# An adaLN block with dilated local attention and a SwiGLU FFN: the second gate moved from w2 to the output tiles, and a new order of all queues

## The chip, the cores and the metric

The kernel runs on one core of one Trainium2 chip. The metric is the device time of one execution in microseconds, as the median over several runs. Before the change it is 240.24 us (three runs, 239.44 to 240.56).

## The reference

`x` is 2048 tokens by 512 features, in bf16. A condition vector `c` gives six modulation rows of 512; a LayerNorm without weights, scaled and shifted, stands ahead of the attention and ahead of the FFN, and each branch is added with a gate.

```python
sa, ca, ga, sb, cb, gb = silu(c) @ w_mod            # six rows of 512
h = layernorm(x) * (1 + ca) + sa
x = x + ga * attention(h, wqkv, wo)
h = layernorm(x) * (1 + cb) + sb
x = x + gb * ((silu(h @ w1) * (h @ w3)) @ w2)       # w1, w3: 512x1792, w2: 1792x512
```

The attention has 32 heads of width 16. Token s sees the 8 tokens s, s-2, ..., s-14; those before token 0 are masked.

## The kernel before

**Tiles.** The tokens are 16 tiles of 128. Weights stay in SBUF. The LayerNorm and projections of the first half run over groups of tiles `LN1 = [[0,1],[2,3],[4..7],[8..11],[12..15]]`, the attention over pairs of tiles, the FFN over groups `FFN = [[0,1],[2,3],[4..7],[8..11],[12,13],[14,15]]`. A group has 256 or 512 tokens.

**The first half.** `ln_stats` takes mean and variance of a tile on VectorE (L555, L556), adds epsilon, raises to -0.5 on POOL (L565) and normalises on VectorE (L576; tile 0 alone by a broadcast operand, L571). In the first group each of the two tiles has its own chain. `ln_T` transposes by TensorE (L636) or, for later groups, by DMA, and applies scale and shift while it evicts to h (L644 on ScalarE, L651 on VectorE, L621 behind a DMA transpose). `proj_qk` and `proj_v` project (L691, L711); for a group with `vh.pieces` each of the four blocks of features is an operation by itself, which can start on its piece of h. v goes to DRAM, so that shifted rows can be loaded.

**Attention of a pair.** `logits`: one VectorE product of 128x4096 per tile (pq, L742) and its sum over features by TensorE (L752). `shift`, `exps`, `softmax`: maximum, exponentials, sum, reciprocal and weights, on VectorE and ScalarE (L764 to L797), and a transpose of the weights (L807, called at). `values`: four loads of shifted v (256 KB each, called vl), one VectorE product of 128x4096 (av, L827), a sum by TensorE (L855, called ac), a copy (L861), a DMA transpose (ot), the output projection with the scaled wo (L867, called wo), and the residual addition, which leaves the row sum too (L871, called rs).

**The FFN.** `ln_sums`: minus the mean on POOL (L586), a Square with its sum on ScalarE per tile (L590), variance, power and bias on POOL (L596, L597, L599), a normalise on ScalarE per tile (L601). `ffn_unit(f)`: gate product (L883), Silu (L889), up product (L883), product of both (hh, L892, VectorE). The text calls these units f0 to f83: 14 per group, f0 to f13 for tiles 0 and 1, f14 to f27 for tiles 2 and 3, f28 to f41 and f42 to f55 for the two groups of 512 tokens, and so on. Units of two groups are interleaved. `ffn_w2` sums over the 14 blocks in two halves of 7 (z0 and z1 are the halves of tile 0, z2 and z3 of tile 1), for the last two tiles in two column halves instead (L909). `store` adds x from PSUM (L931, called zo) and writes out.

**The gates.** ga is multiplied into wo once (L946). gb is multiplied into w2 once, in four parts (L952), so that the w2 sum needs no more than the addition of x.

**What sets the order.** Every operation is recorded first, with its readers and writers. `ORDER` is a written list of all operations; `place` splits it into the queue of each engine, and each engine executes its queue in that order. `SLOTS` gives each temporary its buffer: PSUM banks (8), shifted-v buffers (three with the one that lies over wqkv), products, hidden blocks. A reader waits on its writers by semaphores, and a new tenant of a buffer on the users of the old one. SP issues almost all the DMAs, in its own queue. PSUM banks are so few that a gate or up product must often wait until the bank's tenant two or three units earlier has been read.

Of the kernel before, what the change touches and what calls it, by code (L numbers as in the profile page):

```python
# [7 lines left out]
ALU = mybir.AluOpType  # L8
# [264 lines left out]
def _build(p, A_x, A_wqkv, A_wo, B_w1, B_w3, B_w2, c, w_mod, out):  # L273
# [275 lines left out]
    def ln_stats(Ts):  # L549
# [15 lines left out]
        p.op("pool", lambda e: e.tensor_tensor(rsn, rsn, bass.AP(cst, 1, [[2, P], [0, n]]), ALU.pow), 600, k, r=[va, vcst],  # L565
             w=[vr])
        vns = []
        for T in Ts:
            vn = Val("xn", xnpool)
            if T == 0:  # L570
                p.op("dve", lambda e, vn=vn, T=T: e.scalar_tensor_tensor(vn.at[:], x_sb[:, T, :], mv[:, T, 0:1], bass.AP(rs, T, [[2 * NT, P], [0, D]]),  # L571
                                                                         op0=ALU.subtract, op1=ALU.mult), 600, ("nm", T),
                     r=[vx[T], vr] + vms, w=[vn])
                vns.append(vn)
                continue
# [33 lines left out]
    def ln_T(which, gi, vns):  # L609
        vh = Val("h", hpool)  # L610
        vh.pieces = [Val(f"h_{ft}") for ft in range(KT)] if not which and not gi else None
# [15 lines left out]
        for half in range(2):  # L627
# [12 lines left out]
            for j in range(2):  # L640
# [233 lines left out]
    vw2s = [Val(f"w2_scaled{g}") for g in range(NG)]  # L874
# [24 lines left out]
    def ffn_w2(T, tt, vhh, zops):  # L899

        if T >= NT - 2:
            n = D // 2
            for q in range(2):
                vz = Val("ps_z", psum)
                o = None
                for a, c in ((0, 10), (10, NF)):
                    def mm(e, q=q, vz=vz, a=a, c=c):
                        for fi in range(a, c):
                            ins = e.matmul(bank(vz)[:, 0:n], vhh[fi].at[:, tt * P:(tt + 1) * P], w2[:, fi, q * n:(q + 1) * n],  # L909
# [3 lines left out]
                    o = p.op("pe", mm, (c - a) * c_mm(n), ("z", 2 * T + q), r=vhh[a:c] + vw2s[0 if a == 0 else 2:3 if a == 0 else 4], part=[vz], after=[o] if o else [])  # L913
# [4 lines left out]
        for q in range(2):  # L918
# [6 lines left out]
            o = p.op("pe", mm, 7 * MM, ("z", 2 * T + q), r=vhh[7 * q:7 * q + 7] + vw2s[2 * q - (q > 0):2 * q + 2], part=[vz], after=[o] if q else [])  # L925
            zops[q].append(o)
        store(T, 0, D, vz)
# [10 lines left out]
    for gi, Ts in enumerate(LN1):  # L938
        vns = [v for pr in ([[T] for T in Ts] if gi == 0 else pairs(Ts)) for v in ln_stats(pr)]
# [10 lines left out]
    for g in range(NG):  # L950
        a, b = cuts[g], cuts[g + 1]
        p.op("dve", lambda e, a=a, b=b: e.tensor_tensor(w2[:, a:b, :], w2[:, a:b, :],  # L952
                                                      bass.AP(gb_bc, 0, [[D, P], [0, b - a], [1, D]]), ALU.mult),
             48 + 274 * (b - a), ("mod", 7 + g), r=[vw2[g], vg[1]], w=[vw2s[g]], lock=True)
# [8 lines left out]
    for gi, Ts in enumerate(FFN):  # L963
        vns = [v for pr in pairs(Ts) for v in ln_sums(pr)]
# [112 lines left out]
```

## Time and profile before

| | us |
|---|---|
| median of three runs | 240.24 |
| the runs | 239.44, 240.24, 240.56 |
| span of the profiled execution, first to last instruction | 237.7 |
| TensorE matmuls, busy union | 229.7 |
| VectorE | 179.4 |
| ScalarE | 138.5 |
| POOL | 29.2 |

The profiled execution is recorded as its span alone, 237.7 us; the median of the runs stands 2.5 above it. Where the text works with the span, it adds these 2.5 at the end. The page of the profile lists busy time per engine, the chain of work that ended last, and groups of instructions by source line; the windows give busy time per stretch, and the timeline gives starts and lengths. A row of the timeline reads: start, length, engine, line, operation, tiles, count, and in brackets the idle time before it and who ended it.

### The profile page before, as it was taken

To read this page: it belongs to the slowest core of one execution; us is meant where nothing else is said; L and a number is where in the kernel's file an instruction comes from. 1 tells how busy PE (TensorE), PEld (TensorE's weight loads), DVE (VectorE), ACT (ScalarE), POOL (GpSimd) and SP (SyncE) were. 2 spreads that over 40 slices of the span, in tenths; PEclk is the share of its full clock that TensorE was granted. 3 is DMA by queue.
4 is the path that set the end of the run, shared out by engine and by line. 5 is a ranking of instruction groups with operands and counts; after the bars stand their busy time and mean duration, and the time that the engine had idled before them with its cause. 6 is when DMAs were issued, how large, how long until landed. Compare 5 with 4: busy or idle time off the path is not lost.

```text
span 237.7 us, 4535 instructions
## 1 busy us (share of the span) xinstructions
PE 229.7 (97%) x1781; PEld 136.2 (57%) x1806; DVE 179.4 (75%) x279; ACT 138.5 (58%) x267; POOL 29.2 (12%) x66
## 2 busy tenths in 40 slices
PE   7999999999999998999999999999999999999995
PEld 4776454445588674664444444444475457485774
DVE  5699999999999989999999999682654403434433
ACT  2289577999978744985865594837473405040300
POOL 4434100013002000240002520012010000000000
PEclk9999999999999999999999999999999999999999
DMA  6999999999999999897981693642203000000202
GB/s 216 372 337 322 158 237 299 208 269 283 353 200 270 243 249 199 173 260 177 247 234 47 182 234 72 154 132 46 67 19 91 3 0 0 6 19 0 70 0 88
DMA packets 46317, 38.85 MB, mean 163 GB/s; under 512 B 21704, under 2 KB 37080, under 8 KB 46296
## 3 DMA queue, kind: packets, MB, share of 16 engines
q1 hardware_dynamic: 46288, 38.56, 66.9%
q8 instruction: 14, 0.23, 0.4%
q14 instruction: 7, 0.06, 0.1%
q10 hardware_dynamic: 8, 0.00, 0.0%
HBM read 29.62 MB, written 4.21 MB: 142 GB/s over the span
## 4 chain that ended last, share of the span: by engine, by line
PE 74%; DMA 8%; DVE 8%; SPq 4%; ACT 3%; issue 2%; ACTq 0%; DVEq 0%
PE pall L883 38%; PE pall L921 18%; DMA sb_x<-in_A_x_dram 5%; PE pall L867 5%; SPq L124 4%; PE pall L691 4%; DMA sb_vsh<-v_scratch_dram 3%; PE pall L909 3%; PE pall L855 2%; PE pall L752 2%; PE pall L711 2%; DVE sb_vsh L827 2%; DVE sb_pq L742 2%; DVE sb_hh L892 1%; ACT sb_h L621 1%
## 5 line engine op out<-in xcount | busy, mean ns | idle before, releaser
L883 PE MATMUL pall<-sb_h,sb_w 128*128 128x256 bf16 (+1 forms) x664 | 101.9, 307 | 1.8 <-DVE sb_hh L892 0.9
L883 PEld LDWEIGHTS pall<-sb_h,sb_w 128*128 128x128 bf16 x672 | 64.8, 98 | 37.2 <-issue 2.8
L889 ACT ACTIVATE sb_sg<-pall 128x256 bf16<-128x256 f32 (+1 forms) x84 | 35.6, 453 | 54.1 <-PE pall L883 53.0
L892 DVE TENSOR_TENSOR sb_hh<-sb_sg,pall 128x256 bf16<-128x256 bf16 (+1 forms) x84 | 39.9, 505 | 34.8 <-PE pall L883 32.7
L921 PE MATMUL pall<-sb_w,sb_hh 128*128 128x512 bf16 x190 | 44.0, 379 | 0.3
L742 DVE TENSOR_TENSOR sb_pq<-sb_q,sb_kT 128x4096 bf16<-128x4096 bf16 x16 | 36.3, 2282 | 0.0
L921 PEld LDWEIGHTS pall<-sb_w,sb_hh 128*128 128x128 bf16 x196 | 19.0, 98 | 21.6 <-DVE sb_hh L892 0.4
L691 PE MATMUL pall<-sb_h,sb_wqkv 128*128 128x512 bf16 (+1 forms) x154 | 30.2, 335 | 0.5 <-issue 0.2
L827 DVE TENSOR_TENSOR sb_vsh<-sb_vsh,sb_al 128x4096 bf16<-128x4096 bf16 x12 | 27.3, 2287 | 2.1 <-DMA sb_vsh<-v_scratch_dram 2.1
L621 ACT ACTIVATE sb_h<-sb_h,sb_modc 128x512 bf16<-128x512 bf16 (+1 forms) x24 | 16.5, 743 | 10.1 <-DMA sb_h<-sb_xn 10.1
L691 PEld LDWEIGHTS pall<-sb_h,sb_wqkv 128*128 128x128 bf16 x160 | 14.7, 98 | 11.8 <-ACT sb_ac L861 0.4
L931 DVE TENSOR_TENSOR sb_o<-pall,sb_x 128x512 bf16<-128x512 f32 (+1 forms) x18 | 11.1, 625 | 10.5 <-PE pall L921 6.8
L711 PE MATMUL pall<-sb_wqkv,sb_h 128*128 128x512 bf16 x62 | 15.5, 379 | 0.2
L867 PE MATMUL pall<-sb_wo,sb_ot 128*128 128x512 bf16 x61 | 15.3, 379 | 0.3 <-issue 0.2
L586 POOL TENSOR_SCALAR sb_nm<-sb_sx 128x2 f32<-128x2 f32 x8 | 1.7, 218 | 105.2 <-DVE sb_x L871 105.1
L644 ACT ACTIVATE sb_h<-pall,sb_modc 128x256 bf16<-128x256 bf16 (+1 forms) x18 | 9.9, 612 | 7.5 <-DVE sb_modc L509 6.5
L861 ACT ACTIVATE sb_ac<-pall 128x512 bf16<-128x512 f32 x16 | 9.5, 595 | 7.2 <-PE pall L855 7.1
L601 ACT ACTIVATE sb_xn<-sb_x,sb_nb,sb_rs 128x512 bf16<-128x512 bf16 x16 | 12.4, 806 | 0.7 <-POOL sb_nb L599 0.6
L871 DVE SCALAR_TENSOR_TENSOR sb_x<-pall,sb_x 128x512 bf16<-128x512 f32 x16 | 10.9, 686 | 1.5 <-PE pall L867 1.3
L590 ACT ACTIVATE sb_xn<-sb_x,sb_nm 128x512 bf16<-128x512 bf16 x16 | 11.4, 714 | 0.7 <-POOL sb_nm L586 0.7
L721 ACT ACTIVATE sb_v<-pall 128x512 bf16<-128x512 f32 x16 | 9.5, 600 | 2.8 <-PE pall L711 2.8
L555 DVE BATCH_NORM_STATS2 sb_st<-sb_x 128x6 f32<-128x512 bf16 x16 | 10.6, 680 | 0.8 <-DMA sb_x<-in_A_x_dram 0.7
(87 smaller groups left out, 208.3 us busy)
## 6 DMA issues: line engine op xcount, KB each, us to landing
sb_vsh<-v_scratch_dram SPq DMA_DIRECT2D x48, 256.0 KB, 5.5
sb_vshx<-v_scratch_dram SPq DMA_DIRECT2D x16, 256.0 KB, 4.6
sb_w<-in_B_w_dram SPq DMA_DIRECT2D x6, 512.0 KB, 7.9
sb_w<-in_B_w_dram SPq DMA_DIRECT2D x6, 384.0 KB, 5.4
v_scratch_dram<-sb_v SPq DMA_DIRECT2D x16, 128.0 KB, 6.4
out_dram<-sb_o SPq DMA_DIRECT2D x14, 128.0 KB, 1.8
sb_wqkv<-in_A_wqkv_dram SPq DMA_DIRECT2D x6, 256.0 KB, 6.3
sb_x<-in_A_x_dram SPq DMA_DIRECT2D x4, 256.0 KB, 6.4
```

The source lines that it names most:

```text
L590: p.op("act", lambda e, vn=vn, T=T: e.activation(vn.at[:], x_sb[:, T, :], ACT.Square, bias=nm[:, T, :], accum_out=var[:, T, :]), c_act(512 ...
L601: p.op("act", lambda e, vn=vn, T=T: e.activation(vn.at[:], x_sb[:, T, :], ACT.Identity, bias=nb[:, T, :], scale=rs[:, NT + T, :]), c_act(5 ...
L621: return e.activation(vh.at[:, ft, 0:n * P], vh.at[:, ft, 0:n * P], ACT.Identity, bias=modc[:, 8 * which + ft:8 * which + ft + 1], scale=m ...
L691: ins = e.matmul(bank(vp)[:, j * n:(j + 1) * n], wqkv[:, t, col:col + P], vh.at[:, t, 0:n], start=(t == ORDER[0] and j == 0), stop=(t == O ...
L711: ins = e.matmul(bank(vp), vh.at[:, t, tt * P:(tt + 1) * P], wqkv[:, t, 2 * D:3 * D], start=(t == ORDER[0]), stop=(t == ORDER[-1]))
L742: return e.tensor_tensor(vp.at[:], in0, in1, ALU.mult)
L827: return e.tensor_tensor(v_w, v_w, a_w, ALU.mult)
L867: ins = e.matmul(bank(vy), vt.at[:, ft, :], wo[:, ft, :], start=(ft == 0), stop=(ft == KT - 1))
L883: ins = e.matmul(bank(vp)[:, 0:n], wt[:, t, fi * P:(fi + 1) * P], vh.at[:, t, 0:n], start=(t == 0), stop=(t == KT - 1))
L889: p.op("act", lambda e: e.activation(vt.at[:, 0:n], bank(vgp)[:, 0:n], ACT.Silu), c_act(n), k, r=[vgp], w=[vt], table="silu")
L892: p.op("dve", lambda e: e.tensor_tensor(vh_.at[:, 0:n], vt.at[:, 0:n], bank(vup)[:, 0:n], ALU.mult), c_dve(n), k, r=[vt, vup], w=[vh_])
L921: ins = e.matmul(bank(vz), vhh[fi].at[:, tt * P:(tt + 1) * P], w2[:, fi, :], start=(fi == 0), stop=(fi == NF - 1))
```

## The change

The multiply of w2 by gb is taken out. For tiles 0 to 13 the finished w2 sum is copied from PSUM by ScalarE, multiplied by gb and added to x on VectorE, both in bf16 in SBUF. For the last two tiles two scaled copies of w2 (blocks 0 to 7 and 8 to 13) are made late, in two shifted-v buffers that are free by then. The first pair of tiles has one joint chain for its statistics, and the second pair's projections are cut by pieces too, with two of its evictions on VectorE.

```diff
-        vns = [v for pr in ([[T] for T in Ts] if gi == 0 else pairs(Ts)) for v in ln_stats(pr)]
+        vns = [v for pr in pairs(Ts) for v in ln_stats(pr)]
...
-            if T == 0:
-                p.op("dve", lambda e, vn=vn, T=T: e.scalar_tensor_tensor(vn.at[:], x_sb[:, T, :], mv[:, T, 0:1], bass.AP(rs, T, [[2 * NT, P], [0, D]]),
-                                                                         op0=ALU.subtract, op1=ALU.mult), 600, ("nm", T),
...
-        vh.pieces = [Val(f"h_{ft}") for ft in range(KT)] if not which and not gi else None
+        vh.pieces = [Val(f"h_{ft}") for ft in range(KT)] if not which and gi < 2 else None
...
-                if not half and not which and gi < 1:
+                if not half and not which and gi < 2:
                     p.op("dve", ev_dve, c_dve(n * P), k, r=[vt, vmod[which][2 * half + j]], part=[vh, vh.pieces[2 * half + j]])
...
-    vw2s = [Val(f"w2_scaled{g}") for g in range(NG)]
+    w2v = [Val(f"w2_scaled{i}", vshpool) for i in range(2)]
...
+            def scaled(fi, q):
+                return w2v[fi // 8].at[:, fi % 8, q * n:(q + 1) * n]
...
-                            ins = e.matmul(bank(vz)[:, 0:n], vhh[fi].at[:, tt * P:(tt + 1) * P], w2[:, fi, q * n:(q + 1) * n],
+                            ins = e.matmul(bank(vz)[:, 0:n], vhh[fi].at[:, tt * P:(tt + 1) * P], scaled(fi, q),
...
-        store(T, 0, D, vz)
+        vo = Val("o", opool)
+        k = ("zo", T)
+        p.op("act", lambda e: e.activation(vo.at[:], bank(vz), ACT.Copy), c_act(512), k, r=[vz], w=[vo])
+        o = p.op("dve", lambda e: e.tensor_tensor(vo.at[:], vo.at[:], gb_bc[:], ALU.mult), 340, k, r=[vg[1]], w=[vo], lock=True)
+        p.op("dve", lambda e: e.tensor_tensor(vo.at[:], vo.at[:], x_sb[:, T, :], ALU.add), 340, k, r=[vx[T]], w=[vo], lead=o, lock=True)
+        finals.append(p.dma(out2d[T * P:(T + 1) * P, :], lambda: vo.at[:], k, (128, 1024), r=[vo], cost=400, store=True))
...
-    for g in range(NG):
-        a, b = cuts[g], cuts[g + 1]
-        p.op("dve", lambda e, a=a, b=b: e.tensor_tensor(w2[:, a:b, :], w2[:, a:b, :],
-                                                      bass.AP(gb_bc, 0, [[D, P], [0, b - a], [1, D]]), ALU.mult),
-             48 + 274 * (b - a), ("mod", 7 + g), r=[vw2[g], vg[1]], w=[vw2s[g]], lock=True)
...
+        if Ts[-1] == NT - 1:
+            for i, (a, b) in enumerate(((0, 8), (8, NF))):
+                p.op("dve", lambda e, i=i, a=a, b=b: e.tensor_tensor(w2v[i].at[:, 0:b - a, :], w2[:, a:b, :],
+                                                                     bass.AP(gb_bc, 0, [[D, P], [0, b - a], [1, D]]), ALU.mult),
+                     48 + 274 * (b - a), ("mod", 7 + i), r=vw2 + [vg[1]], w=[w2v[i]], lock=True)
```

`ORDER` and `SLOTS` are new as a whole. Read as queues, SP issues its transfers in the old order up to the third part of w3 (load 19); behind that, and on TensorE, VectorE, ScalarE and POOL, the order differs. The parts of the new queues that the prediction uses:

| tiles | VectorE behind the residual, before | after | TensorE from the last output projection of the group's tiles to its first gate product, after |
|---|---|---|---|
| 0, 1 | sm2 sum, sm2 reciprocal, sm2 weights, sm4 sum, pq7, pq6 | sm2 sum, reciprocal, weights, pq7, pq6 | q17 k16 k17 v13 at2 q16 k18, transposes, k19, transposes, q19 v14 q18, f1 |
| 2, 3 | sm6 weights, w2 scaling, f12 f7 f8 f9 f11 f13, av5 | f5 f12 f10 f3 f11 f9, pq9, f8 f7, pq8 | at6 f12 f12 f10 f3 f9 f9 f8 f7 f8, z2, transposes, f13, z0, f24 |
| 6, 7 | sm8 weights, f18 f14, pq11 | f19 f22, pq11, f24 f27, pq10 | at8 f22 f24 z3 f27 f27 z6 z7 z4 z5 lg10 lg11 ac9 ac8, f32 |
| 8, 9 | f39 f36, av11 | pq15, pq14 | (tiles 10, 11 close the group) f30 f30 f40 f34 wo10 wo11 lg15 lg14 f28 f31 follow wo9 |
| 12, 13 | f48, av14 | zo3, f53, zo0, av14 | f53 f43 f45 f43 f51 f45 f52 ac14 f47 f47 z9 z11 z13, f59 |

Here q, k, v with a number are projections, lg the logits of a tile, sm the softmax steps of a pair.

More of the change, by code (lines that the diff above doesn't have):

```diff
@@ L908, in mm @@
                         for fi in range(a, c):
[L909 removed]
+                            ins = e.matmul(bank(vz)[:, 0:n], vhh[fi].at[:, tt * P:(tt + 1) * P], scaled(fi, q),
                                            start=(fi == 0), stop=(fi == NF - 1))
                         return ins
[L913 removed]
+                    o = p.op("pe", mm, (c - a) * c_mm(n), ("z", 2 * T + q), r=vhh[a:c] + (w2v if a == 0 else w2v[1:]), part=[vz], after=[o] if o else [])
                 store(T, q * n, n, vz)
@@ L923, in mm @@
                 return ins
-            o = p.op("pe", mm, 7 * MM, ("z", 2 * T + q), r=vhh[7 * q:7 * q + 7] + vw2s[2 * q - (q > 0):2 * q + 2], part=[vz], after=[o] if q else [])
+            o = p.op("pe", mm, 7 * MM, ("z", 2 * T + q), r=vhh[7 * q:7 * q + 7] + vw2[2 * q - (q > 0):2 * q + 2], part=[vz], after=[o] if q else [])
             zops[q].append(o)
-        store(T, 0, D, vz)
+        vo = Val("o", opool)
[4 more added lines that the diff above has]
+        finals.append(p.dma(out2d[T * P:(T + 1) * P, :], lambda: vo.at[:], k, (128, 1024), r=[vo], cost=400, store=True))
     def store(T, c0, n, vz):
```

5 lines of the change are left out of this document (1 added, 4 removed), and 134 rows, old and new, of tables (ORDER, SLOTS).

## The prediction

> **What bounds the kernel now.** I read the busy line of the page first, then the windows of 10 us, then the chain of waits, then the timeline at the stalls.
>
> ```profile
> PE 229.7 (97%) x1781; PEld 136.2 (57%) x1806; DVE 179.4 (75%) x279; ACT 138.5 (58%) x267; POOL 29.2 (12%) x66
> ```
>
> ```profile
> 0.00:10.00 10.00, 8.07 (x79) 5.70 (x80) 6.84 (x26) 2.16 (x3) 4.42 (x20) 1.00 0.84 283
> ...
> 80.00:90.00 10.00, 9.13 (x99) 6.44 (x88) 8.82 (x9) 4.31 (x11) 0.00 (x0) 1.00 1.17 239
> 90.00:100.00 10.00, 9.59 (x70) 5.19 (x70) 9.86 (x19) 7.49 (x14) 0.62 (x4) 1.00 0.80 183
> ...
> 170.00:180.00 10.00, 9.95 (x69) 6.67 (x69) 4.46 (x11) 7.67 (x17) 1.31 (x4) 1.00 0.14 45
> ...
> 230.00:238.00 8.00, 5.02 (x47) 4.26 (x44) 2.30 (x5) 0.00 (x0) 0.00 (x0) 0.99 0.21 66
> ```
>
> TensorE is the bound, at full clock (the 1.00), and the change takes no matmul from it. It is idle 8.0 us of 237.7: 1.9 in the first 10 us, 3.0 after the last matmul, 1.3 between 80 and 100, and 1.8 in all the rest. So what can be won is small: the 1.3 us, part of the start, a few tenths. What can be lost is not bounded: TensorE executes its queue in the order that was written, and every late operand is a hole. The chain gives the prices of its work:
>
> ```profile
> 79.47 0.55 PE pall L752 x16
> 80.03 0.43 PE pall L855 x6
> 80.46 0.22 PE pall L636 x2
> 80.67 1.51 PE pall L921 x7
> 82.19 2.62 PE pall L883 x24
> ```
>
> A gate or up product of a 256-token group (4 matmuls) takes 2.62/6 = 0.44, one of a 512-token group 4 x 1.51/7 = 0.86, a half w2 sum 1.51, a logits or value reduction 0.55 each (0.43 x 8/6 for the latter). The 1.3 us look like this in the timeline:
>
> ```profile
> 87.14 2.29 DVE L827 TENSOR_TENSOR sb_vsh<-sb_vsh,sb_al 128x4096 bf16<-128x4096 bf16 x1 [1.04 <-DMA sb_vsh<-v_scratch_dram]
> 89.36 1.40 DVE L892 TENSOR_TENSOR sb_hh<-sb_sg,pall 128x256 bf16<-128x256 bf16 x4
> 89.82 1.05 PE L883 MATMUL pall<-sb_h,sb_w 128*128 128x256 bf16 x8 [0.87 <-DVE sb_hh L892]
> ```
>
> VectorE waited 1.04 for a shifted-v load, four SwiGLU products stood behind that multiply, and TensorE had no free PSUM bank for 0.87 us. Rows on such loads, and on the issue of two transposes, are needed below:
>
> ```profile
> sb_vsh<-v_scratch_dram SPq DMA_DIRECT2D x48, 256.0 KB, 5.5
> ...
> sb_w<-in_B_w_dram SPq DMA_DIRECT2D x6, 384.0 KB, 5.4
> ```
>
> ```profile
> 166.63 2.58 SPq L124 DMA_TRANSPOSE sb_h<-sb_xn  x2
> ```
>
> **The change part by part.**
>
> ```profile
> L952 DVE TENSOR_TENSOR sb_w<-sb_w,sb_gb_bc 128x2048 bf16<-128x2048 bf16 (+1 forms) x4 | 4.3, 1084 | 0.0
> ...
> L931 DVE TENSOR_TENSOR sb_o<-pall,sb_x 128x512 bf16<-128x512 f32 (+1 forms) x18 | 11.1, 625 | 10.5 <-PE pall L921 6.8 <-PE pall L909 3.8
> ...
> L742 DVE TENSOR_TENSOR sb_pq<-sb_q,sb_kT 128x4096 bf16<-128x4096 bf16 x16 | 36.3, 2282 | 0.0
> ...
> L861 ACT ACTIVATE sb_ac<-pall 128x512 bf16<-128x512 f32 x16 | 9.5, 595 | 7.2 <-PE pall L855 7.1
> ```
>
> *Scaling and stores.* The four L952 multiplies (4.3 us, between 68 and 96 us) leave VectorE where it is full; two multiplies over the same 14 blocks return after the last value multiply, again about 4.3, on an engine that is busy 4.5 of 10 us there. For 14 tiles one add from PSUM becomes a ScalarE copy (0.60, the L861 row) and two bf16 operations of 512: a line through the products (4096 wide, 2282 ns) and the mean scaling (1792 wide, 1084 ns) gives 152 ns fixed and 266 per 512, so 0.42 each. So VectorE gets 14 x (0.84 - 0.62) = 3.1 us and ScalarE 14 x 0.60 = 8.4 us more, nearly all after 105 us, where both have room: no cost by themselves (if a copy stands ahead of a needed Silu, 0.6 a time). The multiply of 2.2 us in front of f60's product holds PSUM banks, but four 512-token products (3.5 us) lie in TensorE's queue for that time. The SP queue has the same stores; the first, zo0, stands ahead of the transposes tr18, and its data are there before theirs. At the end zo13's copy, multiply and add lie beside the last 56 half-width matmuls, and the final add and store are unchanged: nothing.
>
> *Start.* Both first tiles now share one power; the broadcast normalise of tile 0 goes.
>
> ```profile
> 5.73 0.74 DVE L571 SCALAR_TENSOR_TENSOR sb_xn<-sb_x,sb_mv,sb_rs 128x512 bf16<-128x512 bf16 x1
> 5.89 1.00 POOL L565 TENSOR_TENSOR sb_rs<-sb_rs,sb_cst 128x1 f32<-128x1 f32 x1 [0.44 <-DVE sb_rs L561]
> 6.93 0.41 DVE L576 TENSOR_SCALAR sb_xn<-sb_x,sb_mv,sb_rs 128x512 bf16<-128x512 bf16 x1 [0.46 <-POOL sb_rs L565]
> ```
>
> Statistics of both, add and one power, put at 0.7, end near 6.3, so tile 0's normalise ends at 6.7 (was 6.47) and tile 1's at 7.1 (was 7.34): the second sets the projections, minus 0.2. Cutting the second pair's projections by feature block and moving two evictions to VectorE lets matmuls start on a part of h: between -0.4 and +0.2 in all, I take -0.2.
>
> *The new order.* This is where the change decides. The transfers up to w3's third group are issued in the old order; behind that, and on all engines, everything moves. I looked at the step that joins attention to the FFN: residual (L871), mean on POOL (L586), two Squares on ScalarE (L590), variance, power and bias on POOL (L596, L597, L599), two normalises on ScalarE (L601), transposes, evictions, first gate matmul. The trace shows what delays it:
>
> ```profile
> 53.31 2.28 DVE L742 TENSOR_TENSOR sb_pq<-sb_q,sb_kT 128x4096 bf16<-128x4096 bf16 x1
> ```
>
> ```profile
> 73.07 0.69 DVE L871 SCALAR_TENSOR_TENSOR sb_x<-pall,sb_x 128x512 bf16<-128x512 f32 x1
> ...
> 77.46 2.28 DVE L827 TENSOR_TENSOR sb_vsh<-sb_vsh,sb_al 128x4096 bf16<-128x4096 bf16 x1
> ```
>
> ```profile
> 52.75 0.19 POOL L596 TENSOR_SCALAR sb_rs<-sb_var 128x2 f32<-128x2 f32 x1 [1.64 <-ACT sb_xn L590]
> 53.03 0.71 POOL L597 TENSOR_TENSOR sb_rs<-sb_rs,sb_cst 128x2 f32<-128x2 f32 x1
> 53.81 1.82 POOL L599 TENSOR_TENSOR sb_nb<-sb_nm,sb_rs 128x2 f32<-128x2 f32 x1
> 73.86 0.22 POOL L586 TENSOR_SCALAR sb_nm<-sb_sx 128x2 f32<-128x2 f32 x1 [18.22 <-DVE sb_x L871]
> 75.72 0.19 POOL L596 TENSOR_SCALAR sb_rs<-sb_var 128x2 f32<-128x2 f32 x1 [1.64 <-ACT sb_xn L590]
> 75.99 0.70 POOL L597 TENSOR_TENSOR sb_rs<-sb_rs,sb_cst 128x2 f32<-128x2 f32 x1
> 76.77 0.20 POOL L599 TENSOR_TENSOR sb_nb<-sb_nm,sb_rs 128x2 f32<-128x2 f32 x1
> ...
> 101.65 1.52 POOL L596 TENSOR_SCALAR sb_rs<-sb_var 128x2 f32<-128x2 f32 x1 [0.70 <-ACT sb_xn L590]
> ```
>
> A POOL operation of 0.20 that begins inside a 2.28 us attention product takes until that product's end: 53.81 + 1.82 = 55.63, just behind 53.31 + 2.28 = 55.59. Outside one it takes 0.20. The power isn't slowed, and the product isn't either (2.28 with a power running at its start). So what counts is which product of 2.28 us follows the residuals in VectorE's queue, and how much work TensorE has between the output projection and the new group.
>
> *Tiles 2 and 3, in full.* Time from the end of wo2. Queue of TensorE after: a transpose pair (0.22), nine products f12 f12 f10 f3 f9 f9 f8 f7 f8 (3.96), z2 (1.51): the transposes are due at 5.7, the first f24 at 8.1. Rows of the same step before:
>
> ```profile
> 74.11 0.72 ACT L590 ACTIVATE sb_xn<-sb_x,sb_nm 128x512 bf16<-128x512 bf16 x1
> ...
> 74.83 0.71 ACT L590 ACTIVATE sb_xn<-sb_x,sb_nm 128x512 bf16<-128x512 bf16 x1
> ...
> 77.00 1.52 ACT L601 ACTIVATE sb_xn<-sb_x,sb_nb,sb_rs 128x512 bf16<-128x512 bf16 x2 [0.62 <-POOL sb_nb L599]
> ```
>
> Residual, mean and two Silus ahead on ScalarE put the Squares at 1.3 to 2.75, the variance at 2.9 (0.18 behind, as 75.54 to 75.72), the power at 3.2 to 3.9, the bias at 4.0. But VectorE's queue is now f9, pq9: f9's Silu follows the Squares at once (2.75 to 3.15), its product runs to 3.6, and pq9 from 3.55 to 5.85 (before, pq9 was long done, and 77.46 was the next long product). The bias ends at 5.9 instead of 4.2, the normalises at 7.4, the transposes wait from 5.9 on: **+1.6**, from 0 (pq9 0.45 later) to 2.0.
>
> *Tiles 8 and 9.* In VectorE's queue pq15 and pq14 stand directly behind rs9. The mean starts 0.1 behind the residual (73.86 against 73.76), pq15 at once: the mean ends with pq15 at 3.0 from the end of wo9, Squares 4.5, the variance with pq14 at 5.2, bias 6.3, normalises 7.8, and the Silu of f30, queued behind them on ScalarE, at 8.4. Its bank passes to f31's gate, due after four 512-token products, two projections, two logits and f28: 3.44 + 1.72 + 1.10 + 0.86 = 7.1. **+1.2**, from 0 to 2.1 (if the exponentials that follow are late as well).
>
> *Tiles 0 and 1.* Before, a reduction of 0.60 stood ahead of pq7, so the variance got in at 52.75, 0.56 ahead of it; now pq7 stands 0.60 earlier and the two meet. Lost race: the variance ends with pq7, the bias with pq6, 2.3 later; the transposes, due behind six projections and a transpose pair (5.4 from wo1's end, 5.3 from the residual's start), wait 2.6. Won: only the bias waits, and they wait 0.7. I take **+1.0**, ends 0.3 and 2.9.
>
> *Tiles 6 and 7, and 12 and 13.* From wo6 to f32 lie 11.7 us of TensorE work (at8, f22, f24, z3, f27 twice, four w2 halves, two logits, two reductions), before 14.3 to f31; pq11 and pq10 fall on the variance and perhaps on the bias: between 0.6 and 2.4 late, I take **+0.7**. From wo12 to f59 lie 12.9, before 16.8 to f56; the long step of av14 falls on the bias: 0.7 to 1.8, I take **+0.7**.
>
> *Loads.* Where the stall at 87 goes, the loads of tile 6 are late next: their buffer comes free with ac5, which TensorE now reaches 4.5 us later, so av6 starts about when ac6 is due. The load of w2's last group is issued behind ot4, about 1.9 from ac4's end (copy 0.6, issue of the transpose 2.58/2), and lands 5.4 later, at 7.3; z1, which needs it, is due 6.1 from ac4's end. Both together 0 to 1.3, I take **+0.4**, since a late TensorE gives the loads time.
>
> Sum against the profiled 237.7: -1.3 (the stall at 80 to 100 goes, with less on VectorE) - 0.2 + 1.6 + 1.2 + 1.0 + 0.7 + 0.7 + 0.4 = +4.1; they overlap in part (what TensorE loses at one step gives loads and VectorE a lead at the next), so I take +3.4, 241.1. The median stands 2.5 above the span: **243.7**.
>
> The Trainium skill (SBUF — State Buffer, "SBUF: two separate sides") states that this port pair is an exclusive lock: a VectorE operation with two SBUF inputs or the GpSimd operation, whichever starts first, holds it for its whole length. The trace agrees for GpSimd as the loser (1.82 against 0.20) and shows no VectorE product held back by the power.
>
> **The rivals.** *POOL keeps its turn* (chance 0.17). If a product that comes during the power waits until the whole POOL step is over, no bias is late: tiles 2 and 3, 6 and 7, 12 and 13 lose nothing, and 243.7 - 1.6 - 0.7 - 0.7 = 240.7. For it: the L571 row, where power and VectorE stretch each other; against it: the row at 53.31, which started inside a power. The Trainium skill's sentence on who starts first (same page and section) would give this time. *Faster* (0.13): every race is won and TensorE's queue covers the steps; the stall at 87 to 93 goes with the scaling, and 240.2 - 1.3 - 0.2 = 238.7. It decides at one place: pq9 starting behind the bias of tiles 2 and 3, not ahead. *Late w2* (0.10): the POOL delays are covered, but z1 waits for the w2 load (1.3) and two copies on ScalarE hold back Silus (1.2): 240.2 + 1.3 + 1.2 - 1.5 = 241.2, near no change. The forecast's own case has 0.60, 241.5 to 247.
>
> **How the numbers follow.** A measurement of this kernel tells about 0.5% (1.2 us) from no change: 239.0 to 241.4. Faster: 0.13. Same: the first rival and most of the third less their tails, 0.17. Slower: 0.70. All low ends give 240.2 - 1.3 - 0.4 + 0.3 + 0.6 + 0.7 = 240.1, all high ends 240.2 - 1.3 + 0.2 + 2.0 + 2.1 + 2.9 + 2.4 + 1.8 + 1.3 = 251.6; the high ends won't all fall together, and I set 239.0 to 247.0, which leaves out the faster case and a little above.
>
> **What would show it.** In the changed profile: L599 of tiles 2 and 3 at 1.5 to 2 us, and TensorE idle ahead of L636 behind it; L586 of tiles 8 and 9 at about 2; windows of 10 us with TensorE at 8 to 9 between 50 and 140, not only 80 to 100; the first projection near 8.0; VectorE clearly under 10 between 60 and 130. The forecast is wrong if L599 stays at 0.20 there, or if TensorE's idle time in the middle is under 3 us.

## The result and the profile after

The changed kernel takes **255.13 us** (four runs, 254.56 to 256.86), the kernel before 239.84 beside it (238.31 to 240.56): 1.065 times as long, 95% interval 1.060 to 1.071. The prediction was 243.7, with a range of 239.0 to 247.0. The profiled execution has a span of 253.2 us, 15.5 more than before.

The busy line of the page after:

```profile
PE 235.3 (93%) x1806; PEld 135.5 (54%) x1806; DVE 181.8 (72%) x292; ACT 144.8 (57%) x279; POOL 34.6 (14%) x65
```

VectorE has 2.4 us more and ScalarE 6.3, somewhat under the 3.1 and 8.4 that the change's operations came to in the prediction; that is not 15 us. The windows of 10 us after (columns: stretch, length, then busy time of TensorE, its weight loads, VectorE, ScalarE, POOL, then the granted clock, the share of the DMA engines and GB/s):

```profile
50.00:60.00 10.00, 6.45 (x36) 2.92 (x34) 8.87 (x13) 4.87 (x11) 5.34 (x4) 1.00 1.01 301
80.00:90.00 10.00, 8.72 (x69) 6.03 (x68) 7.89 (x10) 6.01 (x15) 2.78 (x3) 1.00 1.07 251
100.00:110.00 10.00, 8.59 (x58) 4.25 (x57) 8.20 (x19) 6.64 (x12) 1.53 (x5) 1.00 1.05 202
...
120.00:130.00 10.00, 7.20 (x34) 2.91 (x35) 8.45 (x8) 9.12 (x13) 0.00 (x0) 0.83 0.70 184
...
140.00:150.00 10.00, 8.80 (x69) 4.00 (x67) 8.01 (x10) 6.54 (x15) 4.33 (x7) 1.00 0.62 154
```

Two of the same stretches before:

```profile
50.00:60.00 10.00, 9.95 (x62) 4.86 (x65) 9.93 (x12) 9.58 (x21) 2.95 (x4) 1.00 1.06 292
120.00:130.00 10.00, 9.79 (x87) 4.64 (x87) 10.00 (x12) 5.36 (x13) 1.19 (x2) 1.00 0.48 135
```

TensorE has holes of 1 to 3.5 us where it had none. POOL is busy for 5.34 us with four operations that take 0.2, 0.2, 0.7 and 0.2 where nothing holds them; most of that time is waiting. The timeline at tiles 0 and 1:

```profile
53.05 2.28 DVE L736 TENSOR_TENSOR sb_pq<-sb_q,sb_kT 128x4096 bf16<-128x4096 bf16 x1
53.16 2.22 POOL L590 TENSOR_SCALAR sb_rs<-sb_var 128x2 f32<-128x2 f32 x1 [1.63 <-ACT sb_xn L584]
...
55.32 2.28 DVE L736 TENSOR_TENSOR sb_pq<-sb_q,sb_kT 128x4096 bf16<-128x4096 bf16 x1
...
55.47 2.70 POOL L591 TENSOR_TENSOR sb_rs<-sb_rs,sb_cst 128x2 f32<-128x2 f32 x1
...
58.25 0.20 POOL L593 TENSOR_TENSOR sb_nb<-sb_nm,sb_rs 128x2 f32<-128x2 f32 x1
...
59.34 0.40 PE L630 MATMUL pall<-sb_ident,sb_xn 128*128 128x128 bf16 x4 [3.46 <-ACT sb_xn L595]
```

The variance (0.19 when free) starts 0.11 behind pq7 and takes to its end. Then the **power**, 0.71 when free, starts 0.15 behind pq6 and takes 2.70. Two products in a row hold two operations of one chain. The same at tiles 2 and 3, where the variance and the power run free and the bias is caught:

```profile
80.70 0.19 POOL L590 TENSOR_SCALAR sb_rs<-sb_var 128x2 f32<-128x2 f32 x1 [1.64 <-ACT sb_xn L584]
80.97 0.71 POOL L591 TENSOR_TENSOR sb_rs<-sb_rs,sb_cst 128x2 f32<-128x2 f32 x1
81.31 2.28 DVE L736 TENSOR_TENSOR sb_pq<-sb_q,sb_kT 128x4096 bf16<-128x4096 bf16 x1
81.76 1.88 POOL L593 TENSOR_TENSOR sb_nb<-sb_nm,sb_rs 128x2 f32<-128x2 f32 x1
...
84.55 0.28 PE L630 MATMUL pall<-sb_ident,sb_xn 128*128 128x128 bf16 x2 [0.86 <-ACT sb_xn L595]
```

At tiles 6 and 7 the hold travels further:

```profile
112.63 2.28 DVE L736 TENSOR_TENSOR sb_pq<-sb_q,sb_kT 128x4096 bf16<-128x4096 bf16 x1
112.96 2.00 POOL L593 TENSOR_TENSOR sb_nb<-sb_nm,sb_rs 128x2 f32<-128x2 f32 x1
115.00 0.81 ACT L595 ACTIVATE sb_xn<-sb_x,sb_nb,sb_rs 128x512 bf16<-128x512 bf16 x1 [2.87 <-POOL sb_nb L593]
115.72 0.58 ACT L805 ACTIVATE sb_al<-pall 128x512 bf16<-128x512 bf16 x1
...
116.33 2.29 DVE L821 TENSOR_TENSOR sb_vshx<-sb_vshx,sb_al 128x4096 bf16<-128x4096 bf16 x1 [1.42 <-ACT sb_al L805]
...
120.43 2.93 ACT L615 ACTIVATE sb_h<-sb_h,sb_modc 128x512 bf16<-128x512 bf16 x4 [2.46 <-DMA sb_h<-sb_xn]
...
120.88 0.61 PE L849 MATMUL pall<-sb_vsh,sb_ind 128*32 128x512 bf16 x8 [1.59 <-DVE sb_vsh L821]
...
123.41 1.04 PE L877 MATMUL pall<-sb_h,sb_w 128*128 128x512 bf16 x2 [1.92 <-ACT sb_h L615]
```

ScalarE stands 2.87 us for the bias. Behind the normalise in its queue is the copy of al, which has nothing to do with the LayerNorm; the value product waits for al, and TensorE for the product (1.59). The other branch, normalise, DMA transpose, scale and shift, ends 1.92 too late for the first gate product. After these two holes the clock falls (windows of 1 us):

```profile
122.00:123.00 1.00, 0.00 (x0) 0.00 (x0) 1.00 (x2) 1.00 (x2) 0.00 (x0) 0.85 0.80 209
123.00:124.00 1.00, 0.59 (x2) 0.29 (x3) 1.00 (x1) 0.98 (x3) 0.00 (x0) 0.50 0.88 289
...
126.00:127.00 1.00, 1.00 (x6) 0.49 (x5) 0.97 (x2) 0.98 (x3) 0.00 (x0) 0.95 0.56 137
```

Seven matmuls start 0.30 to 0.43 apart instead of 0.216, which loses 1.3 us in all. At tiles 8 and 9 the mean is caught by pq15, at 12 and 13 the bias by av14; ScalarE stands and a Silu, or a copy that frees a PSUM bank, comes late:

```profile
139.82 4.49 DVE L736 TENSOR_TENSOR sb_pq<-sb_q,sb_kT 128x4096 bf16<-128x4096 bf16 x2
140.00 2.19 POOL L580 TENSOR_SCALAR sb_nm<-sb_sx 128x2 f32<-128x2 f32 x1 [25.04 <-DVE sb_x L865]
...
142.22 0.72 ACT L584 ACTIVATE sb_xn<-sb_x,sb_nm 128x512 bf16<-128x512 bf16 x1 [3.38 <-POOL sb_nm L580]
...
147.52 7.94 PE L877 MATMUL pall<-sb_h,sb_w 128*128 128x512 bf16 x36 [1.20 <-ACT sb_sg L883]
```

```profile
177.31 2.19 POOL L593 TENSOR_TENSOR sb_nb<-sb_nm,sb_rs 128x2 f32<-128x2 f32 x1
...
179.54 0.81 ACT L595 ACTIVATE sb_xn<-sb_x,sb_nb,sb_rs 128x512 bf16<-128x512 bf16 x1 [1.91 <-POOL sb_nb L593]
180.26 0.58 ACT L927 ACTIVATE sb_o<-pall 128x512 bf16<-128x512 f32 x1
...
180.89 0.61 PE L849 MATMUL pall<-sb_vsh,sb_ind 128*32 128x512 bf16 x8 [1.37 <-ACT sb_o L927]
```

The account, from the starts of the matmuls (every place behind 10 us where the next one starts over 0.25 later than its predecessor's width explains; a few pieces of 0.3 to 0.4 in the trace before are matmuls whose records are missing, 1781 of 1806, and are left out):

| where (us) | what was late | lost | before |
|---|---|---|---|
| 55.5, 59.5 | tiles 0, 1: variance and power | 3.9 | 0 |
| 83.3, 84.6 | tiles 2, 3: bias | 1.6 | 0 |
| 118.9, 121.1 | tiles 6, 7: bias, through al and through h | 3.8 | 0 |
| 123.4 to 126.2 | half clock | 1.3 | 0 |
| 145.9 | tiles 8, 9: mean | 1.4 | 0 |
| 155.1 | softmax weights of tiles 12, 13 | 0.7 | 0 |
| 179.1 | tiles 12, 13: bias | 1.5 | 0 |
| 48.0, 76.0, 100.0, 102.3 | transposes (0.5, 1.0) and loads (0.3, 0.8) | 2.5 | 1.6 (88.7, 92.4) |
| sum | | 16.7 | 1.6 |

The difference is 15.1 of the 15.5 us. A hold alone makes no hole: the kernel before has five of them too (POOL operations of 1.52 to 2.10 us at 53.81, 101.65, 129.03, 131.99 and 159.52), and none of the holes in its column stands behind one, since TensorE had other work for that time.

### The profile page after: what moved, and what is told of

The parts are those of the page before. It is cut to its first block, busy times and chain, and to the rows that moved or that the text cites. A ratio compares the mean times of both kernels' runs of the same rounds, so it can differ in the third digit from the quotient of the medians.

```text
span 253.2 us, 4586 instructions
## 1 busy us (share of the span) xinstructions
PE 235.3 (93%) x1806; PEld 135.5 (54%) x1806; DVE 181.8 (72%) x292; ACT 144.8 (57%) x279; POOL 34.6 (14%) x65
## 4 chain that ended last, share of the span: by engine, by line
PE 41%; ACT 5%; POOL 3%; DVE 2%; DMA 1%; issue 1%; SPq 0%
PE pall L877 22%; PE pall L919 12%; PE pall L907 2%; PE pall L861 2%; ACT sb_xn L584 2%; DMA sb_h<-sb_xn 1%; ACT sb_xn L595 1%; PE pall L849 1%; ACT sb_h L615 1%; POOL sb_nb L593 1%; POOL sb_nm L580 1%; POOL sb_rs L591 1%; DVE sb_x L865 1%; ACT pall L776 0%; SPq L124 0%
## 5 line engine op out<-in xcount | busy, mean ns | idle before, releaser
L877 PE MATMUL pall<-sb_h,sb_w 128*128 128x256 bf16 (+1 forms) x672 | 103.8, 311 | 3.3 <-ACT sb_h L615 1.9
L685 PE MATMUL pall<-sb_h,sb_wqkv 128*128 128x512 bf16 (+1 forms) x160 | 30.9, 337 | 0.2
L580 POOL TENSOR_SCALAR sb_nm<-sb_sx 128x2 f32<-128x2 f32 x8 | 3.8, 478 | 133.7 <-DVE sb_x L865 133.7
L705 PE MATMUL pall<-sb_wqkv,sb_h 128*128 128x512 bf16 x64 | 16.1, 379 | 0.0
L638 ACT ACTIVATE sb_h<-pall,sb_modc 128x256 bf16<-128x256 bf16 (+1 forms) x16 | 8.8, 620 | 6.8 <-DVE sb_modc L509 5.7
L927 ACT ACTIVATE sb_o<-pall 128x512 bf16<-128x512 f32 x14 | 8.2, 596 | 5.5 <-PE pall L919 5.5
L695 ACT ACTIVATE sb_kT<-pall 128x512 bf16<-128x512 f32 x16 | 9.3, 602 | 2.7 <-PE pall L685 2.6
L849 PE MATMUL pall<-sb_vsh,sb_ind 128*32 128x512 bf16 x96 | 7.4, 383 | 3.6 <-DVE sb_vsh L821 2.2
```

Source lines behind the costliest of these rows:

```text
L685: ins = e.matmul(bank(vp)[:, j * n:(j + 1) * n], wqkv[:, t, col:col + P], vh.at[:, t, 0:n], start=(t == ORDER[0] and j == 0), stop=(t == O ...
L705: ins = e.matmul(bank(vp), vh.at[:, t, tt * P:(tt + 1) * P], wqkv[:, t, 2 * D:3 * D], start=(t == ORDER[0]), stop=(t == ORDER[-1]))
L877: ins = e.matmul(bank(vp)[:, 0:n], wt[:, t, fi * P:(fi + 1) * P], vh.at[:, t, 0:n], start=(t == 0), stop=(t == KT - 1))
```

## The experiments

**Theory:** POOL's short operations wait for products of VectorE that the new order puts over them, and the holes are these waits, carried on by queues that execute in order. **Rivals:** the new order is late of itself (loads, transposes, less work to cover the steps), or the gate's copies and multiplies cost what is lost. Times are medians, ratios are to the kernel before, run beside.

**1 and 4: POOL's operations on ScalarE.**

```diff
-        p.op("pool", lambda e: e.tensor_scalar(nm[:, i:i + n, 0], sx[:, i:i + n, 0], -1.0 / D, None, op0=ALU.mult), 215, k,
+        p.op("act", lambda e: e.activation(nm[:, i:i + n, 0], sx[:, i:i + n, 0], ACT.Copy, scale=-1.0 / D), 215, k,
...
+        p.op("act", lambda e: e.activation(rsn, var[:, i:i + n, 0], ACT.Identity, bias=cst[:, 0:1], scale=1.0 / D), 210, k, r=vvs + [vcst],
...
+                ins = e.activation(nb[:, j, :], nm[:, j, :], ACT.Copy, scale=rs[:, NT + j, :])
```

> The changed kernel, with the mean, the variance (scale and epsilon) and the bias of the second LayerNorm on ScalarE instead of POOL; the power stays on POOL. Theory (POOL operations that start inside a 2.28 us product wait for its end, and ScalarE's queue waits with them): of the holes in TensorE's work, 2.0 of the 3.9 us at tiles 0 and 1 go (the power can still be held once), all 1.6 at tiles 2 and 3, about 1.8 of 3.8 at tiles 6 and 7 and the 1.5 us at half clock behind them, all 1.4 at tiles 8 and 9 and all 1.5 at tiles 12 and 13; sum 9.8, less up to 1 us for some 30 more short operations on ScalarE: span near 244, time 246 (243 to 249). Rival (the new order itself is late: loads, DMA transposes and ScalarE copies): the holes stay where they are, time 253 to 257.

> The kernel before, with mean, variance and bias of the second LayerNorm on ScalarE as in the first run. Theory: five POOL operations there were held by 1.3 to 1.9 us, but behind cover; without them nothing on TensorE's path changes much: 239.5 (238 to 241). Rival (these holds cost the kernel before too): 237 or less; rival (the extra ScalarE operations cost): 242 or more.

Measured: 254.7 us for the changed kernel so edited (1.068, 1.064 to 1.072) and **249.3 for the kernel before** (1.046, 1.042 to 1.051). Both forecasts of the theory failed, and the second says why the first did. In POOL's queue the place of the mean hardly mattered, since only the other operations of its own chain stood behind it. The same place in ScalarE's queue did (groups by line of the kernel before so edited; the last columns are idle time ahead, and who ended it):

```profile
L586 ACT ACTIVATE sb_nm<-sb_sx 128x2 f32<-128x2 f32 x8 | 1.7, 208 | 8.5 <-DVE sb_x L878 8.5
```

ScalarE stood 8.5 us for residuals. The largest hole of TensorE, 4.0 us ahead of 119.95, has more behind it: the variance of tiles 6 and 7 comes late in ScalarE's queue (108.05), the power, still on POOL, is then held (2.38 at 108.42), and around the end of the hole the clock is at half, from 118.3 to 125.1, which loses 2.6 us. Run 1 tells nothing about the theory.

**5, 6 and 7: the same with the places mended.** In `ORDER` the mean goes directly ahead of its first Square, the variance behind the second, the bias ahead of the first normalise; run 6 cuts the eight products of run 2 as well.

> As the first run (mean, variance and bias on ScalarE), but each of the three moved in the order to where ScalarE needs it: the mean directly ahead of its first Square, the variance directly behind the second Square, the bias directly ahead of the first normalise, so that no other work of ScalarE stands behind an operand that is not there yet. Theory (holds by products make the holes; the first run only put them on another queue): only the power can still be held, about 2 us at tiles 0 and 1 and under 1 at tiles 6 and 7; of the 15.5 us of holes and 1.5 us at half clock some 9 go: 246 (243 to 249). Rival (the order's transfers and copies make the holes): 253 to 257.

> The kernel before with the three operations on ScalarE at the places described. Theory (its holds of 1.3 to 1.9 us lie behind cover, and what slowed the earlier try was ScalarE standing at the early places in its queue): 238.5 (237.5 to 240). Rival (ScalarE cannot take the 40 short operations): 242 or more.

> The same with the eight holding products in quarters too, so that the power is held no more than 0.7 us either. What is left above the kernel before is then the new order's and the gate's own. Theory: 243 (241 to 246), holes of TensorE between 10 us and the end under 6 us in all. Rival (the holds are a symptom, the order itself is late): 246 or more, no better than the quarters alone.

Measured: 249.4 (1.044, 1.038 to 1.051), 241.4 (1.011, 1.003 to 1.020) and 248.0 (1.037, 1.030 to 1.044). All three forecasts were missed on the high side. The 40 short operations cost the kernel before about 1.1% (0.3 to 2.0), more than forecast, and the changed kernel gets 2.1 points back in spite of them: without their price some 3.2 points, 7.7 us, if that price is the same in the new order. The forecast of 243 for run 6 was missed by 5; its profiled execution loses 1.7 us to a stretch at half clock (118.4 to 121.8). With the same 1.1% taken off it stands at 2.5% above.

**2: the holding products in quarters.**

```diff
+                m = W // PIECES.get(("pq", T), 1)
+                for w in range(0, W, m):
...
+                    ins = e.tensor_tensor(vp.at[:, w:w + m], in0, in1, ALU.mult)
```

> The changed kernel, with the eight products that stood over a slow POOL operation (pq6, pq7, pq9, pq10, pq11, pq14, pq15, av14) each written as four products of a quarter, nothing else changed. Theory: a wait on POOL ends with the quarter it starts in, so no POOL operation of 0.20 us takes over 0.9 us and no power over 1.4; holes shrink by about half, VectorE does 3.7 us more in all: time 248 (245 to 252). Rival one (POOL is late for a reason of its own, or waits for the whole row of products): POOL operations of 2 us remain, time 255 to 260. Rival two (the order's transfers): 255 to 259, with short POOL operations.

Measured: **246.5** (1.036, 1.030 to 1.042). The timeline at tiles 0 and 1:

```profile
53.25 2.49 DVE L739 TENSOR_TENSOR sb_pq<-sb_q,sb_kT 128x1024 bf16<-128x1024 bf16 x4
53.36 0.62 POOL L591 TENSOR_SCALAR sb_rs<-sb_var 128x2 f32<-128x2 f32 x1 [1.63 <-ACT sb_xn L585]
54.06 1.03 POOL L592 TENSOR_TENSOR sb_rs<-sb_rs,sb_cst 128x2 f32<-128x2 f32 x1
...
56.69 0.40 PE L631 MATMUL pall<-sb_ident,sb_xn 128*128 128x128 bf16 x4 [0.61 <-ACT sb_xn L596]
```

The variance takes 0.62 instead of 2.22, the power 1.03 instead of 2.70, TensorE's wait is 0.61 instead of 3.46, at the same place in every queue. The hold is no longer than the piece, and a cut product takes 2.49 instead of 2.28. Counted as in the account above, run 2's trace has 8.4 us of holes instead of 16.7: 1.0 left at tiles 0 and 1, none at 2 and 3, 3.0 at 6 and 7 without the half clock, 1.0 at 8 and 9, 0.5 at 12 and 13, and 0.7 and 2.2 for the softmax weights and the loads and transposes, which had 0.7 and 2.5.

**9: the products moved, nothing added.**

```diff
+    for prod, first in ((prods[9], chain[2]), (prods[11], chain[6]), (prods[15], means[8]), (prods[14], chain[8]), (avs[14], chain[12])):
+        prod.deps[first] = True
```

> The changed kernel with seven products moved in VectorE's queue and no operation added: pq7 and pq6 behind the maximum and subtraction of sm4, pq9 behind f8 and f7; pq9, pq11, pq14 and av14 wait for the bias of the LayerNorm that they stood over, pq15 for the mean. Theory (holds make the holes): POOL's short operations take 0.2 us nearly everywhere, the holes at tiles 0 to 3, 8, 9 and 12, 13 and most of those at tiles 6 and 7 go with the 1.5 us at half clock, against up to 3 us of waiting by VectorE: 246 (243 to 249). Rival (the order is late for other reasons): 252 to 257.

The lines shown make five of the products wait; the moves themselves are in `ORDER`.

Measured: 247.2 (1.032, 1.027 to 1.038). No POOL operation behind 45 us takes over 0.75; tiles 0 and 1 as an example:

```profile
53.37 0.19 POOL L592 TENSOR_SCALAR sb_rs<-sb_var 128x2 f32<-128x2 f32 x1 [1.63 <-ACT sb_xn L586]
53.65 0.71 POOL L593 TENSOR_TENSOR sb_rs<-sb_rs,sb_cst 128x2 f32<-128x2 f32 x1
54.43 0.20 POOL L595 TENSOR_TENSOR sb_nb<-sb_nm,sb_rs 128x2 f32<-128x2 f32 x1
```

The hole there is gone, at no price in that place: pq7 and pq6 only changed places with two short operations. Elsewhere part came back: 1.7 us at 83.6, where a SwiGLU product now stands behind pq9 and pq8 (4.49 us), and 1.3 at 137.9, where pq14 waits 1.15 for the bias.

**12: the better cure at each place.**

> The changed kernel with the better of the two cures at each place: pq7 and pq6 behind the maximum and subtraction of sm4, pq9, pq10, pq11, pq14, pq15 and av14 in quarters, no wait added. Theory (two causes: the holds, about 9 of the 15 us, and a new order that leaves the chains to the FFN less time, which no cure of the holds touches): a little better than either cure, 245.5 (243.5 to 247), with the hole near 115 us ahead of the first gate product of tiles 4 to 7 still there at 1.5 to 2.2 us. Rival (the holds were all, the cures were only incomplete): 242 or less, and that hole under 0.5 us.

Measured: 246.9 (1.031, 1.026 to 1.036; runs from 244.7 to 248.4), the span of the profiled execution 242.7. That is inside the range, but within the noise no better than either cure by itself (1.036 and 1.032). The hole ahead of the first gate product of tiles 4 to 7 is still there:

```profile
115.78 1.47 PE L884 MATMUL pall<-sb_h,sb_w 128*128 128x512 bf16 x6 [1.70 <-ACT sb_h L616]
```

Four cures, by ScalarE, by size, by order and mixed, end at 3.1 to 3.6% above the kernel before (run 5 at 3.3 without the price of run 7), from 6.5; run 6, two cures at once, at 2.5 without that price. **So the holds with what follows them are half to two thirds, 7 to 10 of 15.3 us.** The rest these cures don't remove, and part of it is their own price, as the 1.7 and 1.3 us of run 9 are.

**13 and 14: the cause put into the kernel before.** `ORDER` has pq8 ahead of f9 instead of behind f10; run 14 has it in quarters.

> The cause put into the kernel before: the product pq8 moved in VectorE's queue from behind f10 to ahead of f9, so that it starts near 76.5 us and stands over the bias of tiles 2 and 3 (0.20 us at 76.77 in the kernel before). Nothing else is changed. Theory: the bias ends with the product near 78.7, 1.8 later, the normalises, transposes and first gate product behind it too, and a new hole of about 1.5 us opens ahead of the transposes; f9, f11, f13 and av5, 2.28 us later, cost some 1 more: 242 (240.5 to 244). Rival (POOL's waits don't reach TensorE here): no hole ahead of the transposes, at most the 1 us of the delayed products, 240.

> The control: the same move, with pq8 in four quarters. VectorE's work lies as in the run beside it (0.2 us more), only a hold ends with a quarter. Theory: the bias ends at most 0.6 us late, the hole ahead of the transposes shrinks to under 0.5, what the delayed products cost stays: 240.5 (239 to 242). Rival (the delayed products are all that costs): the same time as the run beside it.

Measured: 240.45 (1.007, 1.004 to 1.010) and 241.6 (1.009, 1.006 to 1.012). The timelines, whole first:

```profile
76.90 2.29 DVE L742 TENSOR_TENSOR sb_pq<-sb_q,sb_kT 128x4096 bf16<-128x4096 bf16 x1
77.25 1.99 POOL L599 TENSOR_TENSOR sb_nb<-sb_nm,sb_rs 128x2 f32<-128x2 f32 x1
...
80.14 0.29 PE L636 MATMUL pall<-sb_ident,sb_xn 128*128 128x128 bf16 x2 [0.95 <-ACT sb_xn L601]
```

```profile
76.64 0.39 POOL L600 TENSOR_TENSOR sb_nb<-sb_nm,sb_rs 128x2 f32<-128x2 f32 x1
...
78.41 0.62 PE L637 MATMUL pall<-sb_ident,sb_xn 128*128 128x128 bf16 x6
...
82.03 0.61 PE L862 MATMUL pall<-sb_vsh,sb_ind 128*32 128x512 bf16 x8 [1.70 <-DVE sb_vsh L833]
```

One product whole: a bias of 1.99 and a hole ahead of the transposes (1.7 us in all by the matmuls' starts). The same product in pieces: 0.39 and no hole there. That is the mechanism, alone. But cutting gains no time (the intervals overlap): with the transposes in time, TensorE comes to the value reduction earlier and waits 1.70 there for av5, which the moved product delays in both runs. The theory had the places right, the rival the time: here two late things side by side cost the later one only.

**3, 8 and 15: the gate's part alone, in the old order.**

```diff
+        p.op("act", lambda e: e.activation(vo.at[:], bank(vz), ACT.Copy), c_act(512), k, r=[vz], w=[vo])
+        o = p.op("dve", lambda e: e.tensor_tensor(vo.at[:], vo.at[:], gb_bc[:], ALU.mult), 340, k, r=[vg[1]], w=[vo], lock=True)
```

> The kernel before with the gate's part of the change alone: w2 not scaled, 14 tiles copied by ScalarE, multiplied and added by VectorE where the old addition stood, two scaled copies of w2 behind f55 and f49 for the last two tiles; the old order otherwise. Theory (the scaling is free and the loss lies in the new order's place of products against POOL): 239.5 (238.5 to 241). Rival (the copies on ScalarE and the late scaling cost what the change lost): 246 or more.

> The kernel before with the gate's part alone, as the third run, but each copy up to three ScalarE operations later, and its multiply and addition one VectorE operation later, so that ScalarE doesn't stand waiting for a w2 sum (14.2 us of idle time in the third run, 5.5 in the changed kernel) with Silus behind it. Theory (the gate's part is free where its copy waits for nothing): 239.5 (238 to 241.5). Rival (ScalarE's 8.4 us more, or the missing addition from PSUM, cost by themselves): 242.5 to 245 as in the third run.

> The kernel before with the gate's part alone once more, as the third run, with the copy of tile 0 alone moved, behind the next Silu and both Squares of tiles 4 and 5, and its multiply and addition one VectorE operation later; the stores stay where they were. Theory (the 5 us of the third run came from ScalarE standing 2.9 us before that one copy, with a Silu and the Squares behind it; the gate's part is free by itself): 239.5 (238 to 241.5). Rival (it costs by itself): 242 or more.

Measured: 243.75 (1.023, 1.017 to 1.028), 255.6 (1.069, 1.062 to 1.076) and 241.7 (1.012, 1.004 to 1.020). In run 3 ScalarE stood for a w2 sum with a Silu and two Squares behind it; in run 8 the stores, later now, stood ahead of shifted-v loads in SP's queue, and the value product waited 4.12. A row of each:

```profile
97.85 0.60 ACT L933 ACTIVATE sb_o<-pall 128x512 bf16<-128x512 f32 x1 [2.93 <-PE pall L925]
```

```profile
165.77 2.29 DVE L827 TENSOR_TENSOR sb_vsh<-sb_vsh,sb_al 128x4096 bf16<-128x4096 bf16 x1 [4.12 <-DMA sb_vsh<-v_scratch_dram]
```

Moving one copy brought 2 to 3 of run 3's 5 us back (the two intervals just overlap). At the best place found the gate's part costs 0.4 to 2.0%; that it is free, as I forecast, isn't borne out, and how much of this is the place isn't settled.

**10 and 11: the gate's work left out in the new order** (gb is not applied; one addition from PSUM per tile instead).

> The changed kernel in its own order with the gate's work left out: gb is not applied at all, w2 is used unscaled, each tile has the one addition from PSUM where the copy or the multiply stood, and the two late scaled copies are gone. Theory (the gate's part is cheap, the holds are the loss): 253.5 (251.5 to 255.5), the long POOL operations as before. Rival (ScalarE's copies and VectorE's late multiplies delay what TensorE needs): 249 or less.

> Both: the seven products moved and the gate's work left out (gb is not applied). What stands above the kernel before is then the rest of the new order and of the start. Theory: 244.5 (242 to 247), about 1.5 under the run with the moved products alone. Rival (the gate's part is the larger share): 241 or less.

Measured: 260.1 (1.083, 1.076 to 1.089) and 254.6 (1.060, 1.053 to 1.066): less work, more time, against both forecasts. The addition stands in VectorE's queue where the copy or multiply stood, and holds PSUM banks until VectorE gets to it:

```profile
131.33 1.25 PE L875 MATMUL pall<-sb_h,sb_w 128*128 128x512 bf16 x3 [3.57 <-DVE sb_o L924]
```

Part of the loss is the clock: the profile of run 10 has three stretches of 3.4 us at half clock and that of run 11 two, with TensorE busy throughout, 1.7 us lost in each. The changed kernel lost 1.3 in this way and run 9 nothing, so the clock makes 3.8 of the 6.2 us between the spans of run 10 and the changed kernel (259.4 and 253.2), and 3.4 of the 8.1 between runs 11 and 9 (253.4 and 245.3). In this order ScalarE's copy, which frees the bank early, is worth more than it costs. The gate's price in the new order can't be read by leaving it out.

**What the rest is.** One piece can be read. From the end of the last output projection of tiles 4 to 7 to their first gate product TensorE had 14.2 us before with 0.5 idle, so 13.7 of work; in the changed kernel 15.2 with 4.1 idle, 11.1 of work; in run 12 13.8 with 2.9 idle, 10.9 again. The chain takes about 14 us even with short POOL operations; the new order gives it 2.7 less cover, and 2.9 are lost there with POOL operations of at most 1.03. This is read off, not tested by a run of its own. By the starts of the matmuls run 12's profile has 2.6 us of holes there, 1.8 in other loads and transposes, 0.7 at the softmax weights, 0.6 behind the mean of tiles 8 and 9, and two of 0.4 and 0.3 near 170 and 177: 6.4 in all against 1.6, which makes 4.8 of the 5.0 us by which its span stands above the one before (242.7 and 237.7). Its median stands 7.7 above: the profiled execution is the quickest of six, and the only one with a mean granted clock of 1.000, where the other five have 0.993. One stretch of 3.4 us at half clock takes that much off the mean, and up to 1.7 us of time. That holes of this kind fall together with the new order's shorter cover is read off the traces; which of the moves makes each stays open. No version beat the kernel before.

## Why the prediction was wrong

The sign, the bound (TensorE), the mechanism in the main and all five places were right; three of the five sizes were not. Of the 12 us by which the span came out above the forecast (15.5 more against 3.4), 4.4 lie at tiles 6 and 7, 2.9 at tiles 0 and 1, and 2.1 in loads and transposes. By its steps:

| step | predicted | measured |
|---|---|---|
| stall at 87 to 93, and late loads | -1.3 + 0.4 | -1.6 + 2.5 |
| start | -0.2 | +0.1 |
| tiles 2 and 3 | +1.6 | +1.6 |
| tiles 8 and 9 | +1.2 | +1.4 |
| tiles 0 and 1 | +1.0 | +3.9 |
| tiles 6 and 7 | +0.7 | +3.8, and +1.3 at half clock |
| tiles 12 and 13 | +0.7 | +1.5 |
| softmax weights of tiles 12 and 13 | none | +0.7 |
| overlap | -0.7 | none |

- *"The power isn't slowed."* **This step failed.** It was drawn from powers that had started before a product or between products. One that starts inside a product waits as the others do: 2.70 against 0.71. At tiles 0 and 1 the race was lost as the text said it could be, by 0.11 us, and pq6 behind pq7 then caught the power, where the text had the bias: 3.9 lost, 1.0 above its own high end. The power is 0.8 of that: with 0.71 behind the held variance the bias would have ended with pq6 near 57.65 (an estimate from the rows above), and it ended at 58.45. The larger part is the race itself, which the text priced at up to 2.9 when lost and took at 1.0.
- *Tiles 6 and 7.* **The term was mis-sized by 4.4 us, the largest miss.** The text had TensorE's cover as 11.7 against 14.3, 2.6 short without any hold, and still took 0.7. It counted the way from bias to h alone. The bias was held 1.8 and the variance 0.7, and of the two ways the one through ScalarE's queue, al, and the value product cost 1.75 by itself; the other 2.1; and the two together let the clock fall.
- *Tiles 12 and 13.* The bias was held as said. What was late was not h but the copy of a w2 sum behind the normalise on ScalarE, which is the gate's own and which I had costed at 0.6 "if a copy stands ahead of a needed Silu", not as a bank that a held normalise keeps.
- *Tiles 2 and 3, tiles 8 and 9.* Worked out queue by queue, and right to 0.2, with the engines named (pq9 on the bias; the mean behind pq15, a Silu late).
- *Overlap and taken values.* Between won and lost races I took the middle or less, and 0.7 off for overlap. All five were lost. Even all the high ends came to 251.6, since the power, the second way and the clock were in none.
- *Loads, start.* The stall at 87 went, but loads and transposes near 48, 76, 100 and 102 cost 2.5. The joint chain put the first projection at 8.29 after, against 8.19; in the other runs it came at 8.07 to 8.69 with the joint chain and at 8.12 to 8.89 without: nothing to be told. The way from span to median, put at 2.5, was 2.0 after the change (255.18 and 253.2). Of the idle time before, 2.7 us lie behind the last matmul (235.0 to 237.7) and not 3.0; nothing hangs on it.
- *Rivals.* "POOL keeps its turn" fell with the biases of 1.9 to 2.2 at three places; "faster" decided at pq9, which started ahead of the bias (81.31 against 81.76); for "late w2" no hole waits for a w2 load.

## What to carry to other kernels

Price a short operation in a latency chain by the longest operation that can hold it, once for every link of the chain, and follow the engine that waits for it: everything behind it in that engine's queue is late too, whatever it belongs to. Two holes close together can cost a third time, by the clock: compare the granted clock of every execution. An order written for one set of operations fits that set: the same places are harmless in one engine's queue and cost 10 us in another's, with what they set off, and even leaving work out made this kernel slower. Before a new order is accepted, list for each step how much work the bound engine has between producer and consumer, old and new; here 13.7 against 11.1 us stood in the prediction, nearly, and was not taken at its word.

## What the runs showed of the hardware

- Every POOL operation of the LayerNorm, the power too, waits while VectorE executes a product with both operands in SBUF, for that instruction only: 2.2 at 2.28, 0.6 at a quarter, 0.32 behind a 0.42 multiply of the gate. It ends 0.05 to 0.07 us behind the product and the power 0.54 to 0.56, in every trace; two that started in the last 0.1 us of a quarter (runs 2 and 12, 0.75 each) were held by the next quarter too. Under a VectorE operation that reads PSUM it runs at once (58.25, 0.20, with 0.69 us of the subtraction of sm4 still to come). The Trainium skill (SBUF — State Buffer, "SBUF: two separate sides") names products with two SBUF inputs as the holders, and the trace agrees; its sentence that whoever starts first shuts the other out for its whole length is not borne out the other way round: pq9 began at 81.31 inside a power (80.97 to 81.68) and took its 2.28.
- By the traces' records of the granted clock it changes on a grid of 3.413 us. In the changed kernel's trace it rose at 6.64, fell at 122.69, 34 steps later, and rose at 126.11; the changes in the other traces lie on such a grid too, each with a start of its own. What counts is TensorE's work inside one step: ten steps with 0.25 to 1.34 us of it ended in half clock (the changed kernel's from 119.28 to 122.69 had 0.6, the others are in runs 1, 4, 6, 8, 10 and 11), and of the steps at full clock none with 1.45 or more did. A hole of 3.5 us (55.9 to 59.3) left the clock at 1.00, since it lay across two steps with 1.46 and 1.82 us of work; in run 10 the same hole lay in one, with 0.65, and the clock fell. Where the grid lies differs from execution to execution. The Trainium skill (TensorE: Matmul & The Clock Gate, "Part 1: The HAM clock gate") says that the clock halves after an idle window of about 3.4 us that runs freely, whatever the kernel does. The traces agree with the window, and show that one with up to 1.3 us of work still counts as idle.
